# Gathered values, later weight loads and shared staging in a block-sparse attention and bilinear feed-forward kernel

## The chip, the cores and the metric

The kernel runs on one core of a Trainium2 chip. The metric is the device time of one execution in microseconds. A core has five engines that run beside each other, each through its own instructions in a fixed order: TensorE (PE, matrix products; its weight loads are shown as PEld), VectorE (DVE), ScalarE (ACT), GpSimd (POOL) and SyncE (SP, which here only issues DMAs). ScalarE and GpSimd issue DMAs too.

## The reference, cut to what matters

```
B, H, S, D = 4, 8, 768, 64                # blocks of 32 rows, 24 blocks
scores = q @ k.T / sqrt(D)
mask   = |bi - bj| <= 1, or bi or bj in (0, 23), or bj sampled for bi (3 of 24)
attn   = softmax(where(mask, scores, -1e9))
x      = (attn @ v) as [B*S, H*D]         # [3072, 512]
out    = ((x @ w_a) * (x @ w_b)) @ w_out  # weights are float64, d_ff = 1536
```

Keys and queries are some 4 times larger than values. A middle block attends to eight blocks: itself and its two neighbours, the first and the last, and three sampled ones. The first and the last block attend to all.

## The kernel before, in words

**Units of work.** A unit is one block of one batch, `attend(b, i)`, or `attend_all(b, i)` for blocks 0 and 23. Eight blocks are a chunk of 256 rows (3 chunks a batch, 12 in all). When a chunk's attention is done, its feed-forward products run: `first_products` (line 1429, 12 groups f of columns a chunk, 24 products each) and `second_products` (lines 1512 to 1514). Chunk 1 comes first, so the first eight units are blocks 8 to 15 of batch 0.

**Batch 0 in f32.** Its keys are loaded whole (`keys`, line 540, four DMAs on ScalarE's queue). Per unit GpSimd copies the eight key blocks into one of two tiles KG (lines 701 to 710; VectorE copies the near ones for the first two units). TensorE makes scores (975, with a mask product at 1120), VectorE the negated maxima (1135) and their product with 1/8 (1139), ScalarE the exponentials (1147), TensorE the transpose (1091), ScalarE its copy (1096), TensorE the sums with values (1043), VectorE the factor (1348 to 1356, tile xs), TensorE another transpose (1380), and ScalarE and VectorE write the chunk's rows xT (1391, 1392).

**Values of batch 0.** `gather_values` and `gather_after` fill one of two tiles VG by DMAs on SP's queue: three neighbour blocks (778), the first and last block when the tile changes batch (780, 781), three sampled ones (783). For the first eight units (`NEAR = 8`) the neighbours come instead by copies (745, `near_values`) from the resident values vp, which `plain_values_in` loads on ScalarE's queue (590) and of which it takes the maximum (600).

**Batches 1 to 3 in two f16 parts.** `keys` and `values` load a pair of heads into one of four places of the tile `stage` (546, 612), take its largest magnitude on ScalarE (558, 618), and scale it by a power of two: `set_scale` is a reduction over partitions on GpSimd (440) and three small VectorE operations (443 to 449). The scaled part and its remainder are made by ScalarE and VectorE (563, 564; 629, 630). Keys are transposed into keysT (573). Values are stored to DRAM (vd, 635) and gathered from there. For values the scale is one for all four pairs of a batch, so each pair keeps its place until all four maxima are known (`values_scale`, 645). Probabilities are split in two parts (1003 to 1010), transposed by DMA into one of three places pt (1187, 1291), and the result is factored (1348 on) and transposed by DMA into xT (1368).

**Weights.** `weights` loads 36 tiles of 512 KB with GpSimd's DMAs (898), at first into places of `stage` and of keysT[1]. `convert` makes f32 of the 64-bit words on VectorE (919, 922, 925), takes the maximum (939), and splits in two parts (946, 947). `weight_scale` sets the factor f1 (958, 961).

**Order.** All of it is written as generators that a planner (`Plan`) runs: each step has an engine, a cost in ns and a rank, and the planner emits the step that it reckons can begin first, weighed by rank. What it emits is each engine's fixed order. So any edit of a step, a cost or a number of places moves instructions on all engines.

```
W_BUFS = 6        RAW_BUFS = 4      VG_BUFS = 2
PT_BUFS = 3       NEAR = 8          KG_BUFS = 2
```

Of the kernel before, what the change touches and what calls it, by code (L numbers as in the profile page):

```python
# [48 lines left out]
LATE = 16  # L49
AT_ONCE = 4  # L50
NEAR = 8
# [243 lines left out]
def kernel(  # L295
# [43 lines left out]
    def take(tag, bufs):  # L339
        return rings.setdefault(tag, Ring(bufs)).take()  # L340
# [11 lines left out]
    stage = kvp.tile([P, RAW_BUFS, 2 * NT * D], F32, name="stage")  # L352
    keysT = [kvp.tile([P, H, S], F16, name=f"keysT{i}") for i in range(2)]
# [16 lines left out]
    n_at = at_g + NC  # L370
    bound = const.tile([P, n_at], F32, name="bound")
    bound_v = const.tile([P, B * NG], F32, name="bound_v")
# [16 lines left out]
    mark = const.tile([1, 1], F32, name="mark")  # L389
    offs = const.tile([1, NB, NR], I32, name="offs")  # L390
# [136 lines left out]
    def raw_tile(b, g, n):  # L527

        yield stage_freed
        t = stage[:, raw_taken[0] % RAW_BUFS]  # L530
        raw_taken[0] += 1
        freed = yield from take("raw", RAW_BUFS)
        return t, freed

    raw_taken = [0]

    def keys(b, g):
# [70 lines left out]
    def values(b, g):  # L608
# [18 lines left out]
        vs = work.tile([P, NT, 2, 2 * D], F16, tag="ks", name=f"vs{b}_{g}", bufs=KS_BUFS)  # L627
        s = scale[:, at_v + b : at_v + b + 1]
# [12 lines left out]

    def values_scale(b):
# [3 lines left out]
            bound[:, at : at + 1], bound_v[:, b * NG : b * NG + (NG if b else NT // 2)],  # L646
# [76 lines left out]

    def plain_vg(n):
# [29 lines left out]
    def gather_after(n):  # L754
        b, i, x = vg_units[n]
        vg_free[n] = yield from take("vg", VG_BUFS)
        if n + 1 < len(vg_units):
            plan.start(gather_values(n + 1), order[vg_units[n + 1][:2]] - LEAD_G)
        to, of, row = VG[n % VG_BUFS], vd[b], ROW
        if b == 0:  # L760
            to, of, row = plain_vg(n), plain_values, H * D
        dense = i in (0, NB - 1)
        first = vg_holds.get(n % VG_BUFS) != b
        vg_holds[n % VG_BUFS] = None if dense else b
# [119 lines left out]
    def weights(n):  # L884

        f, i = divmod(n, 3)
        if n == 0:
            yield from gate(W_GATE)
# [64 lines left out]
    def weight_scale(f):  # L953
# [670 lines left out]
```

## Time and profile before

| | |
|---|---|
| median of three executions | 807.28 us (803.25, 807.28, 808.39) |
| the profiled execution's own time | 803.08 us |
| its span, first to last instruction | 801.3 us |
| mean granted TensorE clock | 0.983 of 2.4 GHz |
| moved by DMA | 131.8 MB, mean 164 GB/s |

The profile shows one execution. Busy times of an engine leave out register, branch, semaphore and DMA-issuing instructions. An operation may begin before the one ahead of it on the same engine has ended, so the distance from one begin to the next is what it takes of the engine. "A <- B" is a wait of A that B ended. Lines are those of the kernel before.

### The profile page before, as it was taken

What the parts mean: (1) busy time and instruction counts of PE and PEld (TensorE: products, weight loads), DVE (VectorE), ACT (ScalarE), POOL (GpSimd) and SP (SyncE); (2) the same over time, 40 slices, a digit from 0 to 9 for tenths busy, and PEclk for the clock granted to TensorE, in tenths of its full rate; (3) what the DMA queues carried; (4) which work ended last, traced back from release to release, by engine and by line L of the source; (5) the groups of instructions that cost most, each with busy time, mean ns of one, the idle gap of its engine ahead of it and who ended that gap; (6) DMA issues with size and microseconds to landing.
All of it is one profiled execution on the core that took longest, in us unless ns stands there. A gap on an engine that the chain in (4) does not pass through costs nothing.

```text
span 801.3 us, 25888 instructions
## 1 busy us (share of the span) xinstructions
PE 742.4 (93%) x10056; PEld 522.5 (65%) x10056; DVE 533.6 (67%) x1504; ACT 490.9 (61%) x1202; POOL 227.6 (28%) x532
## 2 busy tenths in 40 slices
PE   2759789899998989999999999999989999999997
PEld 0426568674567748757758758658658757768853
DVE  5899999975666677676577686667667775322132
ACT  2666888786656677776466686565566664333333
POOL 5535833212233432202233432302234320000001
PEclk9879999999999999999999999999999999999999
DMA  8776786865577899897579998968687788310001
GB/s 270 234 215 196 228 249 189 266 131 135 126 186 163 182 197 226 179 231 155 144 180 170 214 239 170 210 172 171 155 179 164 147 158 167 91 34 1 2 1 53
DMA packets 184135, 131.80 MB, mean 164 GB/s; under 512 B 135627, under 2 KB 155724, under 8 KB 184012
## 3 DMA queue, kind: packets, MB, share of 16 engines
q1 hardware_dynamic: 170860, 82.89, 50.3%
q0 software_dynamic: 11616, 44.05, 17.5%
q10 hardware_dynamic: 1536, 3.21, 1.3%
q8 instruction: 79, 1.29, 0.7%
q14 instruction: 44, 0.36, 0.2%
HBM read 87.63 MB, written 11.01 MB: 123 GB/s over the span
## 4 chain that ended last, share of the span: by engine, by line
PE 65%; DVE 13%; DMA 9%; issue 5%; ACT 4%; SPq 3%; POOL 0%; POOLq 0%; ACTq 0%; DVEq 0%
PE ab L1429 37%; PE o L1512 6%; PE o L1514 5%; PE o L1513 5%; PE av L1043 5%; PE s L984 4%; DMA VG<-vd 4%; DMA vd<-vs 2%; DMA vp<-in_v_dram 2%; DVE low L1135 1%; SPq L666 1%; DVE wab L947 1%; SPq L783 1%; PE s L1120 1%; PE s L975 1%
## 5 line engine op out<-in xcount | busy, mean ns | idle before, releaser
L1429 PE MATMUL ab<-xT,wab 128*128 128x256 f16 x3456 | 393.2, 273 | 2.8 <-DVE g L1448 2.1
L1429 PEld LDWEIGHTS <-wab 128*128 128x128 f16 x3456 | 332.8, 98 | 58.1 <-issue 16.9
L1448 DVE TENSOR_TENSOR g<-g,ab 128x256 f32<-128x256 f32 x144 | 60.4, 419 | 112.9 <-ACT g L1445 109.3
L1445 ACT ACTIVATE g<-ab,f 128x256 f32<-128x256 f32 x144 | 67.7, 470 | 104.2 <-PE ab L1429 103.2
L1483 DVE SCALAR_TENSOR_TENSOR gh<-g,scale,gh 128x256 f16<-128x256 f32 x144 | 69.5, 494 | 72.0 <-ACT gh L1482 70.9
L1482 ACT ACTIVATE gh<-g,scale 128x256 f16<-128x256 f32 x144 | 70.7, 504 | 74.5 <-PE o L1514 70.6
L1512 PE MATMUL o<-wo,gh 128*128 128x512 f16 x288 | 110.1, 382 | 0.0
L1513 PE MATMUL o<-wo,gh 128*128 128x512 f16 x288 | 109.5, 380 | 0.0
L1514 PE MATMUL o<-wo,gh 128*128 128x512 f16 x288 | 109.5, 380 | 0.0
L710 POOL COPY KG<-keysT 128x128 int32 (+1 forms) x264 | 89.0, 375 | 44.6 <-POOL KG L701 22.5
L701 POOL COPY KG<-keysT 128x384 int32<-128x384 int32 (+1 forms) x86 | 50.6, 589 | 164.6 <-PE s L984 146.0
L1147 ACT ACTIVATE sm<-s,low,cq 128x256 f32<-128x256 f32 x132 | 73.6, 559 | 31.7 <-DVE low L1141 15.6
L440 POOL PARTITION_ALL_REDUCE power<-bound x58 | 25.8, 447 | 180.1 <-DVE bound L1462 103.7
L1043 PE MATMUL av<-VG,pt 128*32 128x128 f16 (+2 forms) x3488 | 63.5, 212 | 13.0 <-DMA VG<-vd 9.4
L1010 DVE SCALAR_TENSOR_TENSOR hl<-sm,hl 128x256 f16<-128x256 f32 (+1 forms) x156 | 69.8, 453 | 1.8 <-ACT hl L1003 0.5
L1135 DVE TENSOR_REDUCE low<-s 128x2 f32<-128x512 f32 x88 | 60.1, 683 | 14.9 <-PE s L984 12.0
L1043 PEld LDWEIGHTS <-pt 128*32 128x32 f16 x2688 | 33.1, 97 | 35.4 <-issue 26.6
L1512 PEld LDWEIGHTS <-gh 128*128 128x128 f16 x288 | 28.2, 98 | 36.9 <-issue 6.0
L1514 PEld LDWEIGHTS <-gh 128*128 128x128 f16 x288 | 28.2, 98 | 34.3 <-issue 0.5
L1513 PEld LDWEIGHTS <-gh 128*128 128x128 f16 x288 | 28.3, 98 | 29.1 <-issue 0.3
L1452 ACT ACTIVATE junk<-g 128x1024 f16<-128x1024 f32 x36 | 38.0, 1055 | 10.4 <-DVE g L1448 10.2
L1006 DVE TENSOR_SCALAR hl<-sm 128x256 f16<-128x256 f32 (+1 forms) x113 | 36.3, 325 | 11.7 <-DMA pt<-hl 8.9
(136 smaller groups left out, 932.3 us busy)
## 6 DMA issues: line engine op xcount, KB each, us to landing
VG<-vd SPq DMA_DIRECT2D x210, 64.0 KB, 3.0
VG<-vd SPq DMA_DIRECT2D x66, 192.0 KB, 3.7
q<-in_q_dram POOLq DMA_DIRECT2D x18, 512.0 KB, 4.9
VG<-vd SPq DMA_DIRECT2D x24, 384.0 KB, 3.7
out_dram<-ou POOLq DMA_DIRECT2D x24, 256.0 KB, 3.6
stage<-in_v_dram POOLq DMA_DIRECT2D x12, 384.0 KB, 4.5
vd<-vs SPq DMA_DIRECT2D x12, 384.0 KB
stage<-in_k_dram POOLq DMA_DIRECT2D x12, 384.0 KB, 6.5
```

What stands on the lines that cost most here:

```text
L710: nc.gpsimd.tensor_copy(to[:, :, (5 + r) * w : (6 + r) * w], of[:, :, bass.ds(at, w)])
L1010: t = yield dve(221 + n * 1.03, lambda: nc.vector.scalar_tensor_tensor(lo, sm, over, hi, ALU.mult, ALU.subtract))
L1043: mm(both[hs, :, i % 2, hq] if two else av[hs, i % 2, hq], pt[:, y, hs], of if two or b == 0 else of[:, 0], start=(i % 2 == 0 and hq == 0 ...
L1135: yield dve(685, lambda: nc.vector.tensor_reduce(mx, ps, axis=mybir.AxisListType.X, op=ALU.max, negate=True))
L1147: t = yield act(750, lambda hq=hq: nc.scalar.activation(sm[:, hq], ps[:, hq], AF.Exp, bias=low[:, at, hq, 0:1], scale=factor_of(b, cc, hq) ...
L1429: mm(ab[:, i, :].rearrange("p (j x q) -> p j x q", j=PER // 2, x=2), wab[:, f, i, part, kt, :], xc[:, :, a, :, kt, :], start=(i == 0 and k ...
L1445: yield act(460, lambda: nc.scalar.activation(g, ab[:, 0, :], AF.Copy, scale=f1[:, f : f + 1]))
L1482: yield act(400, lambda: nc.scalar.activation(gh[:, 0], g, AF.Copy, scale=s))
L1483: t = yield dve(480, lambda: nc.vector.scalar_tensor_tensor(gh[:, 1], g, s, gh[:, 0], ALU.mult, ALU.subtract))
L1512: mm(po, gh[:, 0, js], wo[:, f, 0], start=(f == 0), stop=False)
L1513: mm(po, gh[:, 0, js], wo[:, f, 1], start=False, stop=False)
L1514: mm(po, gh[:, 1, js], wo[:, f, 0], start=False, stop=(f == NF - 1))
```

## The change

- `NEAR = 0`: the neighbour values of the first eight units come by DMA gathers (778) like all others; `near_values` is no longer called.
- The first weight load waits until the second key tile has landed: a one-element GpSimd copy (`mark_w`) stands ahead of it.
- For batch 0 the product of the maxima with 1/8 goes from VectorE to ScalarE. f1 is made by one VectorE operation in place of two.
- Each pair of value heads has a scale of its own, set as soon as its own maximum is known. `values_even` takes the largest of the four and makes factors, `evened`, that the attention result's divisor takes in.
- `stage` has two places for keys and values in place of four. The room behind them is a third place for gathered values of batches 1 to 3, and a fourth for transposed probabilities.

```diff
+RAW_PLACES = 2
-NEAR = 8
+NEAR = 0
...
+    spare = stage.rearrange("p g x -> p (g x)")[:, RAW_PLACES * 2 * NT * D :]
...
-        t = stage[:, raw_taken[0] % RAW_BUFS]
+        t = stage[:, raw_taken[0] % RAW_PLACES]
-        freed = yield from take("raw", RAW_BUFS)
+        freed = yield from take("raw", RAW_PLACES)
...
+            if g == 1:
+                k_early.fire(t)
...
+        at = at_p + (b - 1) * NG + g
-            t, AF.Abs, accum_out=bound_v[:, b * NG + g : b * NG + g + 1],
-        ))
+            t, AF.Abs, accum_out=bound[:, at : at + 1],
+        ))
+        end = yield from set_scale(slice(at, at + 1))
         v_bound[b].fire(end)
         if g == NG - 1:
-            plan.start(values_scale(b), order[b, 0] - LEAD_V)
-        yield v_scale[b]
+            plan.start(values_even(b), order[b, 0] - LEAD_V)
...
-        s = scale[:, at_v + b : at_v + b + 1]
+        s = scale[:, at : at + 1]
...
+    def values_even(b):
+
+        yield v_bound[b]
+        at, to = at_p + (b - 1) * NG, at_v + b
+        yield dve(150, lambda: nc.vector.reduce_max(
+            rscale[:, to : to + 1], rscale[:, at : at + NG], axis=mybir.AxisListType.X
+        ))
+
+        def factors():
+            for x in range(2):
+                ps = slice(x * D, (x + 1) * D)
+                nc.vector.tensor_scalar(
+                    evened[ps, b], scale[ps, at : at + NG].rearrange("p (a i) -> p a i", i=2)[:, :, x],
+                    rscale[ps, to : to + 1], float(2.0 ** 14), ALU.mult, ALU.mult,
+                )
+
+        end = yield dve(320, factors)
+        v_scale[b].fire(end)
...
+    def split_vg(m):
+        at = vg_at[m]
+        if at < VG_BUFS:
+            return VG[at]
+        return spare[:, :ROW].bitcast(F16).rearrange("p (a x) -> p a x", a=2)
+
+    n_plain = sum(u[0] == 0 for u in vg_units)
+    vg_at = [m % VG_BUFS if m < n_plain else (m - n_plain) % 3 for m in range(len(vg_units))]
...
         if n == 0:
-            yield from gate(W_GATE)
+            yield k_early
+            yield pool(120, lambda: nc.gpsimd.tensor_copy(mark_w, plain_keys[0:1, 1, 0:1]))
...
-        end = yield dve(160, lambda: nc.vector.tensor_mul(
-            f1[:, f : f + 1], rscale[:, at : at + 1], rscale[:, at + 2 : at + 3]
-        ))
-        end = yield dve(160, lambda: nc.vector.tensor_mul(
-            f1[:, f : f + 1], f1[:, f : f + 1], rscale[:, at + 1 : at + 2]
+        end = yield dve(165, lambda: nc.vector.scalar_tensor_tensor(
+            f1[:, f : f + 1], rscale[:, at : at + 1], rscale[:, at + 1 : at + 2],
+            rscale[:, at + 2 : at + 3], ALU.mult, ALU.mult,
         ))
...
-            yield dve(165, lambda: nc.vector.tensor_scalar(mx, mx, D ** -0.5, None, ALU.mult))
+            yield act(200, lambda: nc.scalar.mul(mx, mx, D ** -0.5))
...
+    def place_pt(name, cols):
+        freed = yield from take("pt_split", PT_BUFS + 1)
+        at = pt_taken[0] % (PT_BUFS + 1)
+        pt_taken[0] += 1
+        if at == PT_BUFS:
+            yield stage_freed
+            t = spare[:, ROW : ROW + 4 * P].bitcast(F16).rearrange("p (a x) -> p a x", x=P)
+            return t[:, :cols], freed
+        return work.tile([P, cols, P], F16, tag="pt", name=f"pt{name}", bufs=PT_BUFS), freed
...
-            yield dve(165, lambda: nc.vector.tensor_scalar(
-                dn, dn, EPS, float(2.0 ** 14), ALU.add, ALU.mult
+            yield v_scale[b]
+            yield dve(165, lambda: nc.vector.scalar_tensor_tensor(
+                dn, dn, EPS, evened[:, b].unsqueeze(1).to_broadcast([P, 2, HQ]),
+                ALU.add, ALU.mult,
             ))
```

Lines in the orders are each kernel's own.

VectorE in the first units, before: 922 and 925 convert weights, 1135 and 1139 make maxima, 745 are the near copies into VG.

```order
L922 SCALAR_TENSOR_TENSOR wab<-keysT_77,wab 128x512
L1135 TENSOR_REDUCE low<-s_288 128x2
L745 COPY VG_84<-vp_115 32x512
L745 COPY VG_84<-vp_150 32x512 x2
L745 COPY VG_85<-vp_150 32x512 x3
L1139 TENSOR_SCALAR low<-low 128x2
L645 TENSOR_REDUCE bound<-bound_v 128x1
L925 SCALAR_TENSOR_TENSOR wab<-keysT_77,wab 128x512
L1135 TENSOR_REDUCE low<-s_319 128x2
L745 COPY VG_85<-vp_150 32x512 x3
L1348 TENSOR_SCALAR den<-den 128x4
```

The same place after: 970, 973 and 976 convert weights, 1184 makes maxima, 1407 and 1414 are the divisor.

```order
L1184 TENSOR_REDUCE low<-s_289 128x2
L970 TENSOR_SCALAR wo<-stage 128x512
L973 SCALAR_TENSOR_TENSOR wo<-stage,wo 128x512
L1407 TENSOR_SCALAR den<-den 128x4
L1184 TENSOR_REDUCE low<-s_317 128x2
L1414 RECIPROCAL den<-den 128x4
L976 SCALAR_TENSOR_TENSOR wo<-stage,wo 128x512
L1417 TENSOR_TENSOR xs_8_397<-av_8_323,den 128x256
L1184 TENSOR_REDUCE low<-s_403 128x2
```

The copies and the scalings of the maxima are gone from between the maxima. At the third and fourth unit's maximum the weights stand at the third tile (wo, from stage) where they stood at the fourth (wab, from keysT).

GpSimd at the start, before: 871 clears the queries' tile, 898 loads weights, 710 gathers sampled key blocks.

```order
L871 MEMSET QZ_112 64x1024 x2
L898 DMA stage<-in_moe_w_a_dram 128x1024
L898 DMA stage<-in_moe_w_b_dram 128x1024
L656 TENSOR_LOAD offs
L710 ISA
L710 COPY KG_82<-keysT_76 128x4x32
```

GpSimd at the start, after: 939 is the one-element copy that waits for the second key tile, 949 loads weights, 738 gathers key blocks.

```order
L921 MEMSET QZ_114 64x1024 x2
L939 COPY mark_w<-keysT_76 1x1
L949 DMA stage<-in_moe_w_a_dram 128x1024
L684 TENSOR_LOAD offs
L738 ISA
L738 COPY KG_82<-keysT_76 128x4x32
```

The second weight load (w_b) has left this place. It stands behind the copies of the first two units.

SP in batch 1, before: 778 and 783 gather values of a unit into VG, 1187 transposes a unit's probabilities, 1368 its output.

```order
L1187 DMA_TRANSPOSE pt_3595<-hl_3515 128x8x128
L778 DMA VG_84<-vd_79 96x1024
L783 ISA
L783 DMA VG_84<-vd_79 32x1024
L783 ISA
L783 DMA VG_84<-vd_79 32x1024
L783 ISA
L783 DMA VG_84<-vd_79 32x1024
L1187 DMA_TRANSPOSE pt_3750<-hl_3657 128x8x128
L1368 DMA_TRANSPOSE xT_86<-xo_0_3752 128x4x128
L778 DMA VG_85<-vd_79 96x1024
```

SP in batch 1, after: 828 and 833 gather values, 1429 transposes an output, 1235 probabilities; the gather into stage uses the third place.

```order
L833 DMA VG_85<-vd_79 32x1024
L828 DMA stage<-vd_79 96x1024
L694 TENSOR_LOAD offs
L833 ISA
L833 DMA stage<-vd_79 32x1024
L833 ISA
L833 DMA stage<-vd_79 32x1024
L833 ISA
L833 DMA stage<-vd_79 32x1024
L1429 DMA_TRANSPOSE xT_86<-xo_0_3719 128x4x128
L1235 DMA_TRANSPOSE stage<-hl_3721 128x8x128
L828 DMA VG_84<-vd_79 96x1024
```

Two gathers follow each other, the second ahead of the transposes, where a gather stood between transposes before.

## Rows read from the trace of the kernel before

**Rows 1.** The page, part 1: busy us, share of the span, instructions.

```profile
PE 742.4 (93%) x10056; PEld 522.5 (65%) x10056; DVE 533.6 (67%) x1504; ACT 490.9 (61%) x1202; POOL 227.6 (28%) x532
```

**Rows 2.** Table by stretch; the first row names the columns, after the stretch's length.

```profile
core 0: us, PE busy (x) PEld busy (x) DVE busy (x) ACT busy (x) POOL busy (x), PEclk, DMA share, GB/s
0.00:12.00 12.00, 0.35 (x4) 0.21 (x4) 3.51 (x22) 1.49 (x2) 3.27 (x8) 1.00 0.85 236
12.00:40.00 28.00, 20.38 (x286) 10.14 (x286) 24.18 (x57) 16.33 (x45) 18.30 (x42) 0.88 0.82 258
40.00:65.00 25.00, 14.85 (x230) 7.76 (x227) 24.46 (x69) 16.25 (x42) 8.28 (x17) 0.73 0.74 221
65.00:120.00 55.00, 46.83 (x780) 33.55 (x781) 54.76 (x134) 44.20 (x120) 34.93 (x68) 0.97 0.74 223
120.00:169.00 49.00, 46.80 (x611) 38.07 (x610) 44.94 (x119) 40.49 (x95) 13.78 (x27) 1.00 0.73 208
169.00:300.00 131.00, 122.20 (x1713) 79.21 (x1711) 87.84 (x262) 85.28 (x213) 42.91 (x109) 1.00 0.72 162
300.00:700.00 400.00, 394.79 (x5752) 285.78 (x5750) 268.50 (x781) 251.68 (x619) 102.19 (x256) 1.00 0.83 177
```

**Rows 3.** Waits of TensorE, 12 to 65 us: total us, times, longest.

```profile
PE av L1380 <- DVE xs L1356: 8.5, 3, 5.2
...
PE s L975 <- POOL KG L710: 4.9, 1, 4.9
```

**Rows 4.** The chain of waits, 12 to 66 us: start, us, what.

```profile
5.58 10.22 DMA vp<-in_v_dram
...
18.91 7.83 DMA vp<-in_v_dram
...
49.87 0.34 DVE wab L919
...
50.63 0.58 DVE wab L922
```

**Rows 5.** Groups of VectorE, 0 to 130 us: count, busy us, mean ns, idle before.

```profile
L745 DVE COPY VG<-vp 32x512 f32<-32x512 f32 x21 | 9.3, 443 | 0.5
```

**Rows 6.** Timeline of VectorE, 44 to 45 us: start, us, what.

```profile
44.24 0.15 DVE L1139 TENSOR_SCALAR low<-low 128x2 f32<-128x2 f32 x1
44.30 0.15 DVE L961 TENSOR_TENSOR f<-f,rscale 128x1 f32<-128x1 f32 x1
```

**Rows 7.** Timeline of GpSimd, 0 to 16 us.

```profile
2.64 0.68 POOL L898 DMA_DIRECT2D stage<-in_moe_w_a_dram  x1
3.32 0.55 POOL L898 DMA_DIRECT2D stage<-in_moe_w_b_dram  x1
12.63 0.88 POOL L710 COPY KG<-keysT 128x128 f32 x3 [8.76 <-DMA keysT<-in_k_dram]
...
15.25 0.53 POOL L898 DMA_DIRECT2D stage<-in_moe_w_out_dram  x1
```

**Rows 8.** The DMA view: 0 to 13 us in 40 slices, its queue q0; whole run's landing.

```profile
GB/s 0 0 0 0 0 2 180 95 255 340 370 360 355 380 321 380 429 385 293 243 230 221 277 233 233 202 271 214 325 217 236 310 241 271 276 331 266 364 389 399
...
q0 software_dynamic: 256, 0.97, 25.6%
...
stage<-in_moe_w_a_dram POOLq DMA_DIRECT2D x4, 512.0 KB, 4.7
```

**Rows 9.** Waits of TensorE, 169 to 700 us.

```profile
PE av L1043 <- DMA VG<-vd: 9.4, 8, 2.4
```

**Rows 10.** Timeline of ScalarE, 0 to 3 us.

```profile
2.04 0.20 ACT L1537 ACTIVATE warm<-warm 128x1 f32<-128x1 f32 x1
```

**Rows 11.** Staging: GpSimd's key loads and SP's value stores (timelines); landing of line 612.

```profile
275.93 1.10 POOL L546 DMA_DIRECT2D stage<-in_k_dram  x2
...
351.91 1.80 SPq L635 DMA_DIRECT2D vd<-vs  x2
...
DMA to landing us min/median/max: 3.7/4.5/5.9
```

More of the change, by code (lines that the diff above doesn't have):

```diff
@@ L369 @@
     at_g = at_w + 3 * NF
-    n_at = at_g + NC
+    at_p = at_g + NC
+    n_at = at_p + (B - 1) * NG
     bound = const.tile([P, n_at], F32, name="bound")
-    bound_v = const.tile([P, B * NG], F32, name="bound_v")
+    bound_v = const.tile([P, NT // 2], F32, name="bound_v")
+    evened = const.tile([P, B, HQ], F32, name="evened")
     power = const.tile([P, n_at], F32, name="power")
@@ L389 @@
     mark = const.tile([1, 1], F32, name="mark")
+    mark_w = const.tile([1, 1], F32, name="mark_w")
     offs = const.tile([1, NB, NR], I32, name="offs")
@@ L529, in raw_tile @@
         yield stage_freed
-        t = stage[:, raw_taken[0] % RAW_BUFS]
+        t = stage[:, raw_taken[0] % RAW_PLACES]
         raw_taken[0] += 1
-        freed = yield from take("raw", RAW_BUFS)
+        freed = yield from take("raw", RAW_PLACES)
         return t, freed
     raw_taken = [0]
+    k_early = Event()
     def keys(b, g):
@@ L645, in values_scale @@
         yield dve(150, lambda: nc.vector.reduce_max(
-            bound[:, at : at + 1], bound_v[:, b * NG : b * NG + (NG if b else NT // 2)],
+            bound[:, at : at + 1], bound_v,
             axis=mybir.AxisListType.X,
@@ L722, in gather_keys, with take_vg @@
         k_free[b].fire(t)
+    def split_vg(m):
[5 more added lines that the diff above has]
+    vg_at = [m % VG_BUFS if m < n_plain else (m - n_plain) % 3 for m in range(len(vg_units))]
+    vg_user = {}
+    def take_vg(m):
+        at = vg_at[m]
+        if at >= VG_BUFS:
+            yield stage_freed
+        ev = Event()
+        last = vg_user.get(at)
+        vg_user[at] = ev
+        if last is not None:
+            yield last
+        return ev
     def plain_vg(n):
@@ L755, in gather_after @@
         b, i, x = vg_units[n]
-        vg_free[n] = yield from take("vg", VG_BUFS)
+        vg_free[n] = yield from take_vg(n)
         if n + 1 < len(vg_units):
             plan.start(gather_values(n + 1), order[vg_units[n + 1][:2]] - LEAD_G)
-        to, of, row = VG[n % VG_BUFS], vd[b], ROW
         if b == 0:
             to, of, row = plain_vg(n), plain_values, H * D
+        else:
+            to, of, row = split_vg(n), vd[b], ROW
         dense = i in (0, NB - 1)
-        first = vg_holds.get(n % VG_BUFS) != b
-        vg_holds[n % VG_BUFS] = None if dense else b
+        first = vg_holds.get(vg_at[n]) != b
+        vg_holds[vg_at[n]] = None if dense else b
         def copies():
@@ L1183, in attend @@
         mine = yield from turn("pt", b, i)
-        kept = yield from take("pt", PT_BUFS)
+        pt, kept = yield from place_pt(f"{n}", 8)
         mine.fire(0)
-        pt = work.tile([P, 8, P], F16, tag="pt", name=f"pt{n}", bufs=PT_BUFS)
         t = yield sp(1300, 1500, lambda: nc.sync.dma_start_transpose(
@@ L1193, in attend @@
         yield from before(b, i)
-        vg = VG[m % VG_BUFS]
+        vg = split_vg(m)
         quads = [
@@ L1286, in attend_quad @@
             freed[x].fire(t)
-            kept = yield from take("pt", PT_BUFS)
+            pt, kept = yield from place_pt(f"{n}_{hq}{x}", 6)
             if x == 1:
                 mine_pt.fire(0)
-            pt = work.tile([P, 6, P], F16, tag="pt", name=f"pt{n}_{hq}{x}", bufs=PT_BUFS)
             t = yield sp(1100, 1130, lambda hl=hl, pt=pt: nc.sync.dma_start_transpose(
@@ L1315, in all_values @@
         else:
-            vg = VG[m % VG_BUFS].rearrange("p a x -> p (a x)")
+            vg = split_vg(m).rearrange("p a x -> p (a x)")
             terms = [
@@ L1329 @@
     ride = [Event() for _ in units]
+    pt_taken = [0]
+    def place_pt(name, cols):
[3 more added lines that the diff above has]
+        if at == PT_BUFS:
+            yield stage_freed
+            t = spare[:, ROW : ROW + 4 * P].bitcast(F16).rearrange("p (a x) -> p a x", x=P)
+            return t[:, :cols], freed
+        return work.tile([P, cols, P], F16, tag="pt", name=f"pt{name}", bufs=PT_BUFS), freed
     quad_sent = {(b, i): Event() for b in range(B) for i in (0, NB - 1)}
```

## The prediction

> **What bounds the kernel now.** I read the page first: TensorE is busy 93% of the span, VectorE 67%, ScalarE 61%, GpSimd 28% [rows 1]. The reader is to see there a kernel that is bound by its matrix products, in which only idle time of TensorE can be won. Both kernels issue the same products (10056 before; the order of after has as many of each kind), so the question is where the 59 us of idle stand (801.3 - 742.4) and who ends them.
>
> The table by stretch says where [rows 2]. TensorE stands idle 11.7 us in 0:12, 7.6 in 12:40, 10.2 in 40:65, 8.2 in 65:120, 2.2 in 120:169, 8.8 in 169:300, 5.2 in 300:700 and 5.8 at the end. So 40 us of 59 lie before 169 us, and in the same rows VectorE is busy 24.5 of 25, 54.8 of 55 and 44.9 of 49 us: from 40 to 169 us VectorE is the bound. It turns the int64 weights into two f16 parts there (36 tiles); the products of the first two chunks wait for the weights and for the attention output, which VectorE makes too.
>
> The waits of TensorE in 12:65 confirm it: 8.5 us for the output factor xs of VectorE, 4.9 us for the first gathered keys, which GpSimd could not copy before 12.6 us [rows 3]. The granted clock is 0.88 and 0.73 of 2.4 GHz in 12:40 and 40:65 [rows 2], so part of the time at 1.2 GHz, after stretches in which TensorE was idle; a higher clock alone would save nothing there, since VectorE sets the end, and I count nothing for it.
>
> Last I read the chain of waits. From 5.6 to 26.7 us it is two loads of the plain values vp [rows 4], and after them mostly VectorE. The near copies of the first eight blocks needed vp.
>
> **The change part by part.** Most of it takes work off VectorE ahead of 169 us.
>
> Near values: 24 copies of 32x512 go, 21 of which VectorE ran in 9.3 us with 0.5 us idle before them [rows 5]: -9.3 us of VectorE. In their place SP issues 8 DMAs of 192 KB (1.57 MB more to move), counted below.
>
> Scaled maxima: 22 small VectorE operations move to ScalarE. Each lasts 0.15 us, but the next begins 0.06 us after it began [rows 6], so one takes some 0.07 us of the engine: -22 x 0.07 = -1.5. The factor f1: one operation in place of two for 12 groups, -12 x 0.07 = -0.8. Scaling the values per head pair: four factors a batch in place of one, three VectorE operations each; up to the last weight the order of after has 10 more of these and the few that even them out: +0.9. The sum on VectorE up to the last weight is -9.3 - 1.5 - 0.8 + 0.9 = -10.7 us.
>
> On ScalarE the 22 operations cost 22 x 0.20 = 4.4 us, by the one row of so small an operation [rows 10]; three near copies go from it. ScalarE is busy 16.3 of 28 and 16.3 of 25 us in the stretches where most stand [rows 2], and the operation stands right ahead of the exponentials on the same engine, so a hop between engines goes as it comes. I take 0; without the cover it costs the 4.4. The Trainium skill (ScalarE: Activation LUTs, Rules for kernel authors) says the contrary: multiplications belong on VectorE, and a short ACTIVATE is budgeted at about 0.3 us; an estimate by that page is 22 x 0.3 = 6.6 us on ScalarE for 1.5 us saved. The trace agrees only in that ScalarE's is the longer operation (0.20 against 0.15).
>
> Weights behind keys: GpSimd now waits for the second key tile before its first weight load. Before, it issued w_a at 2.64 and w_b at 3.32 us, then stood until 12.63 and sent w_out at 15.25 [rows 7]; 0.97 MB of weights moved by 13 us, while the keys were landing [rows 8]. Behind the waiting instruction stand, in GpSimd's order, the load of w_a, the gathers of the first two key blocks, and only then w_b. At the some 300 GB/s of these slices 0.97 MB is 3.2 us: the keys land some 2.5 us earlier (not all of 3.2, since w_a follows the second key tile), at about 10 us, and with them the first scores. w_b then goes out 2.6 us later (12.63 to 15.25 for the same copies), at about 12.5 in place of 3.3 us, and lands after 4.7 us [rows 8] at 17; w_out follows at 21. So VectorE has less to do between 10 and 28 us: three tiles, of one operation of 0.34 and two of 0.58 us each [rows 4], are 4.5 us, and attention's own operations I estimate at as much again; that is 9 of 18 us, and 9 idle. Before, it was busy 24.2 of 28 us in 12:40, which is 2.5 idle in 18. The difference of 6.5, less 2.5 for the earlier keys, is +4. The bounds are 0 (the early tiles were not missed) and +9 (the whole delay of w_b). The 1.57 MB of gathers are 5 us at the same rate, in stretches where the DMA engines are 82% and 74% busy [rows 2]; that they hide is part of the 4, and that they don't is in the 9.
>
> The start therefore gains 10.7 - 4 = 6.7 us. What is late next there is VectorE still: it works 124 of the 129 us from 40 to 169 [rows 2].
>
> Values scaled per pair, GpSimd: 9 more small reductions over 500 us, on an engine busy 28%: 0. With them a pair is written out as soon as its own maximum is known, which lets a staging place go sooner; that pays for taking two of the four places away. I take 0 for both together; the price if it doesn't is below.
>
> Two more places: the room becomes a third place for gathered values and a fourth for transposed weights of attention. Between 169 and 700 us TensorE waits 9.4 us in 8 waits for gathered values [rows 9]; with a third place the gather of a block goes out a block earlier. The third pair of orders above shows a gather that no longer stands behind a transpose. The bounds are -9.4 and 0; some of these waits are SP's own queue, which is no shorter, so I take -4, a little under the middle. For the fourth place I take 0: among TensorE's waits I found none that it would end.
>
> **The sum.** -6.7 - 4.0 = -10.7 us. Against the profiled execution's own 803.08 us (span 801.3 and 1.8 around it) that is 792.4. The median of the three runs shown, 807.28, is 4.2 us above the profiled one; against it the sum gives 796.6. I forecast **796.5 us**. A measurement of this kernel tells about 1% (8 us) from no change.
>
> **The rivals.**
>
> *The gain at the start is given back.* The late weights and the 1.57 MB of gathers starve VectorE for the full 9 us, so 1.7 of its 10.7 remain; and the waits for gathered values were SP's queue, so a third place gives 2. Time: 807.3 - 3.7 = 803.6. For it: w_b goes out 9 us later, and the DMA engines are 82% busy in 12:40 [rows 2]. Against it: GpSimd's loads were held back by VectorE later on anyway, so a tile missed early is made up only if VectorE has idle time, which it hadn't after 40 us; and the chain up to 27 us [rows 4], the loads of vp, is gone.
>
> *Slower: two staging places hold up the next batch.* From the first key load of a batch to its last stored values it took 76 us, 275.9 to 351.9, for eight tiles through four places [rows 11]. Through two places each tile must turn within 76 / 4 = 19 us. A tile lands after 4.5 us [rows 11], and its five steps on three engines wait behind other work, since each engine keeps a fixed order. From 19 us a tile on, the next batch is late: at 22 us by 4 x 3 = 12 us, at two changes of batch 24 us, and 807.3 - 10.7 + 24 = 820.6. For it: the order of after loads the last two value tiles of a batch behind the first key gathers of that batch. Against it: the 76 us held the wait for all four maxima, which goes, and no wait of TensorE for keys or values at a change stands out now.
>
> *ScalarE's extra operations are on the path.* Each unit's chain then grows by 0.20 us at a place that nothing covers: 22 x 0.20 = 4.4 us, and 796.6 + 4.4 = 801.0. This is the rule of the Trainium skill above, at the trace's price. Against it: ScalarE is over a third idle there [rows 2].
>
> **How the numbers follow.** The forecast case gets 0.64, the gain given back 0.20, the two staging places 0.11, ScalarE 0.05. The forecast's own range is 791 to 803: VectorE's idle between +1 and +7, and the third place between -7 and -1, about its 796.6. Of its 0.64, 0.08 lies within 1% (above 799.2); the gain given back and ScalarE lie within 1% altogether; the two staging places are slower. So faster 0.56, same 0.33, slower 0.11. The range 786 to 809 leaves out the slower case and little else, under 0.2: its low end has both open terms at their best (10.7 + 9.4 = 20.1 off 807.3, and 1 more), its high end the gain given back with 5 us of gathers that don't hide.
>
> **What would show it.** Right: GpSimd's first key gather at about 10 us in place of 12.63; no near copy on VectorE; the last weight part on VectorE at about 162 us (before, the stretch that ends at 169 us ends with it); TensorE idle before that point down by 5 to 8 us; its waits for gathered values under 6 us. The late weights would show as VectorE idle of over 17 us in 0:40 (12.3 before). Wrong: VectorE full as before and the last weight where it was; new waits of TensorE for keys or gathered values at 330 to 360 and 500 to 530 us, when batches change; GpSimd standing before a load of keys or values.

## The result, and the profile after

The changed kernel takes 817.82 us (median of six, 811.49 to 826.18) against 807.32 us (median of six, 803.00 to 808.39): 1.0104 of the time before, 95% interval 1.006 to 1.0149; the ratio leaves out the execution of 826.18, which was in a slow state. The forecast was 796.5, its range 786 to 809. The profiled execution took 812.58 us, its span 810.8 (803.08 and 801.3 before).

Page, part 1, of the kernel after:

```profile
PE 742.2 (92%) x10056; PEld 525.0 (65%) x10056; DVE 516.3 (64%) x1469; ACT 496.3 (61%) x1234; POOL 228.4 (28%) x542
```

TensorE's work is that of [rows 1]; VectorE has 17.3 us less. The 9.5 us of span are idle time of TensorE, and the mean granted clock is 0.983 in both. The table by stretch of the kernel after says where it stands:

```profile
0.00:12.00 12.00, 0.35 (x4) 0.21 (x4) 4.28 (x25) 1.49 (x2) 3.51 (x11) 1.00 0.84 250
12.00:40.00 28.00, 19.84 (x310) 11.13 (x310) 16.87 (x37) 17.11 (x55) 17.68 (x43) 0.92 0.96 261
40.00:65.00 25.00, 16.62 (x275) 9.62 (x271) 23.72 (x61) 18.14 (x48) 10.63 (x20) 0.75 0.92 279
65.00:120.00 55.00, 48.10 (x759) 35.84 (x748) 52.99 (x122) 44.56 (x127) 32.87 (x67) 0.97 0.74 213
120.00:169.00 49.00, 46.33 (x603) 35.81 (x602) 43.56 (x117) 41.35 (x99) 14.72 (x27) 1.00 0.83 240
169.00:300.00 131.00, 119.73 (x1751) 79.20 (x1754) 89.74 (x265) 85.12 (x210) 45.27 (x113) 0.99 0.74 163
300.00:700.00 400.00, 385.50 (x5637) 279.40 (x5625) 256.41 (x776) 249.42 (x619) 99.74 (x256) 1.00 0.84 175
```

Against [rows 2]: up to 169 us TensorE's idle time went from 39.8 to 37.8 us, 2 us won where 6.7 were forecast. From 169 to 700 us it went from 14.0 to 25.8, 11.8 lost. VectorE's work up to 169 us fell by 10.4 us (151.85 to 141.43; forecast 10.7), but in 12:40 it is busy 16.9 of 28 us (24.2 before), and the DMA engines 96% and 92% in 12:40 and 40:65 (82% and 74%).

The DMA view of the kernel after (line's tiles, count, KB each, median us to landing), then its timelines of GpSimd and VectorE:

```profile
stage<-in_moe_w_a_dram POOLq DMA_DIRECT2D x4, 512.0 KB, 9.1
```

```profile
11.38 0.88 POOL L738 COPY KG<-keysT 128x128 f32 x3 [5.25 <-DMA keysT<-in_k_dram]
...
170.09 0.74 DVE L998 SCALAR_TENSOR_TENSOR wo<-w,scale,wo 128x512 f16<-128x512 f32 x1
```

The four loads of w_a into stage that landed in 4.7 us [rows 8] now need 9.1, and the last weight part ends at 170.8 us (168.8 before, forecast about 162). The first gather of keys moved only from 12.63 [rows 7] to 11.38. VectorE is idle 18.8 us in 0:40, over the 17 that were to show the late weights.

The last weight part before (VectorE's timeline of the kernel before), then a load of vp that is still in the chain of waits of after:

```profile
168.06 0.75 DVE L947 SCALAR_TENSOR_TENSOR wo<-w,scale,wo 128x512 f16<-128x512 f32 x1
```

```profile
8.92 9.62 DMA vp<-in_v_dram
```

Waits of TensorE after, 12:65 (first fence) and 169:700 (second):

```profile
PE av L1092 <- DMA VG<-in_v_dram: 7.0, 3, 3.7
...
PE s L1024 <- POOL KG L738: 4.1, 1, 4.1
PE av L1441 <- DVE xs L1417: 2.6, 2, 1.9
```

```profile
PE av L1092 <- DMA pt<-hl: 6.3, 8, 1.2
PE av L1092 <- DMA stage<-hl: 6.0, 3, 2.7
PE ab L1490 <- DVE g L1509: 5.2, 5, 1.7
```

At the start the waits for xs [rows 3] fell by 6 us and waits for gathered neighbours took their place. Later the 9.4 us for gathered values [rows 9] are gone, and 12.3 us of waits for transposed probabilities stand there. Before, the same view has:

```profile
PE av L1043 <- DMA pt<-hl: 0.5, 1, 0.5
PE ab L1429 <- DVE g L1448: 0.2, 1, 0.2
```

So SP's transfers together cost TensorE 12.3 us in place of 9.9. All waits of the view sum to 26.0 us in place of 13.6; the other 10 us of the difference are waits for VectorE (the feed-forward tile g above all, 5.2 against 0.2) and for ScalarE (6.5 against 2.0).

### The profile page after: what moved, and what is told of

It reads as the page before. It is cut to its first block, busy times and chain, and to the rows that moved or that the text cites. A ratio compares the mean times of both kernels' runs of the same rounds, so it can differ in the third digit from the quotient of the medians.

```text
span 810.8 us, 25904 instructions
## 1 busy us (share of the span) xinstructions
PE 742.2 (92%) x10056; PEld 525.0 (65%) x10056; DVE 516.3 (64%) x1469; ACT 496.3 (61%) x1234; POOL 228.4 (28%) x542
## 4 chain that ended last, share of the span: by engine, by line
PE 57%; DMA 15%; DVE 12%; ACT 6%; issue 6%; POOL 1%; SPq 1%; POOLq 0%; ACTq 0%
PE ab L1490 33%; PE o L1573 5%; PE o L1575 5%; PE o L1574 5%; PE av L1092 4%; PE s L1033 3%; DMA stage<-in_v_dram 3%; DMA pt<-hl 3%; DMA stage<-hl 2%; DMA keysT<-ks 2%; DMA vp<-in_v_dram 1%; DVE low L1184 1%; PE s L1024 1%; ACT sm L1196 1%; DVE g L1509 1%
## 5 line engine op out<-in xcount | busy, mean ns | idle before, releaser
L729 POOL COPY KG<-keysT 128x384 int32<-128x384 int32 (+1 forms) x86 | 48.4, 563 | 173.5 <-PE s L1033 149.3
L445 POOL PARTITION_ALL_REDUCE power<-bound x67 | 29.9, 448 | 211.5 <-DVE bound L1523 102.6
L1092 PE MATMUL av<-VG,pt 128*32 128x64 f32 (+2 forms) x2160 | 42.3, 220 | 11.5 <-DMA VG<-in_v_dram 7.0
L1513 ACT ACTIVATE junk<-g 128x1024 f16<-128x1024 f32 x36 | 38.0, 1057 | 12.2 <-DVE g L1509 11.9
L1055 DVE TENSOR_SCALAR hl<-sm 128x256 f16<-128x256 f32 (+1 forms) x100 | 30.8, 313 | 15.8 <-DMA stage<-hl 10.2
L1092 PEld LDWEIGHTS <-pt 128*32 128x32 f16 x2032 | 24.9, 97 | 24.7 <-issue 14.6
```

What stands on the lines that cost most here:

```text
L1092: mm(both[hs, :, i % 2, hq] if two else av[hs, i % 2, hq], pt[:, y, hs], of if two or b == 0 else of[:, 0], start=(i % 2 == 0 and hq == 0 ...
```

## The experiments

All ratios are to the kernel before, with a 95% interval. The theories, by the letters that the expectations use: **T**, the third place lets the planner put gathers ahead of transposes in SP's queue, and TensorE waits for these. **S**, the gathers fill the DMA engines at the start, and VectorE waits for loads instead of working less. **G**, the wait ahead of the first weight starves VectorE. **P**, any edit makes the planner write a new order, and a new order alone gives or costs about a per cent.

| run | ratio | interval | TensorE idle 0:169 | 169:700 |
|---|---|---|---|---|
| before | 1 | | 39.8 | 14.0 |
| after | 1.0104 | 1.0060 to 1.0149 | 37.8 | 25.8 |
| e1 | 1.0073 | 1.0038 to 1.0108 | 38.2 | 26.7 |
| e2 | 1.0015 | 0.9978 to 1.0053 | 40.5 | 18.7 |
| e3 | 1.0115 | 1.0076 to 1.0153 | 39.0 | 22.6 |
| e4 | 0.9971 | 0.9936 to 1.0007 | 37.7 | 19.8 |
| e5 | 0.9958 | 0.9926 to 0.9991 | 43.0 | 15.6 |
| e6 | 1.0102 | 1.0042 to 1.0161 | 36.4 | 25.9 |
| e7 | 0.9944 | 0.9890 to 0.9998 | 38.1 | 19.1 |
| e8 | 1.0038 | 1.0002 to 1.0074 | 38.6 | 25.4 |
| e9 | 1.0179 | 1.0130 to 1.0228 | 37.3 | 32.4 |
| e10 | 1.0072 | 1.0033 to 1.0111 | 34.4 | 25.4 |
| e11 | 1.0117 | 1.0082 to 1.0152 | 38.7 | 30.3 |
| e12 | 1.0189 | 1.0134 to 1.0244 | 39.3 | 29.6 |
| e13 | 0.9962 | 0.9932 to 0.9991 | 38.3 | 20.3 |
| e14 | 1.0030 | 0.9997 to 1.0063 | 40.0 | 22.9 |
| e15 | 1.0039 | 1.0008 to 1.0069 | 39.7 | 19.3 |
| e16 | 0.9974 | 0.9941 to 1.0007 | 38.7 | 16.2 |
| e17 | 1.0365 | 1.0312 to 1.0418 | 45.3 | 41.2 |
| e18 | 0.9972 | 0.9936 to 1.0008 | 37.9 | 16.0 |

Idle is 169 or 531 us less TensorE's busy time in the table by stretch. How far to trust it: e5 turned out to have the order of before on every engine, so it is a repeat of before, and came out at 0.9958, its idle time up to 169 us 3.2 us off. Differences under 0.5%, and of some 3 us in one profile's start, are not read below.

### The parts of the start (e1, e2, e3)

```diff
-NEAR = 0
+NEAR = 8                        # e1, e3
-            yield k_early
-            yield pool(120, lambda: nc.gpsimd.tensor_copy(mark_w, ...
+            yield from gate(W_GATE)     # e2, e3
```

> The changed kernel with NEAR = 8 again: near values by copies, all else changed. Theory S (the start is bound by DMA, which the gathers fill): DMA share in 12 to 65 us falls from 0.94 to under 0.85, weight loads land in 5 to 6 us in place of 8 to 9, but VectorE has its 9.3 us of copies again; last weight part at 167 to 171 us (170.8 in the changed kernel), time 808 to 816. Theory G (the late first weight load alone starves VectorE): landings and DMA share stay, last weight at 178 or later, time 820 or more.

> The changed kernel without the wait of the first weight load for the second key tile. Theory G (the wait costs VectorE its early tiles): VectorE's idle in 0 to 40 us falls from 18.9 to 14 or less and the last weight part comes at 163 to 166 us in place of 170.8; time 6 to 8 us under the changed kernel's. Theory S (DMA is full in 12 to 65 us whatever goes first): the early tiles come sooner, later ones later; last weight within 2 us of 170.8, time within 3 us of the changed kernel's.

> The changed kernel with both edits of the start undone (near copies back, no wait for keys); per-pair scaling, maxima on ScalarE, two more places stay. The start should be that of the kernel before, less 2 us of small VectorE operations: last weight at 165 to 169 us. If the middle (169 to 700 us) costs what the trace shows (idle 20.6 us against 14.0 before), the time is 5 to 9 us over the kernel before all the same; if the start alone is to blame, it is within 3 us of it.

The two undone parts do not add up: alone they give -0.3% and -0.9% against after, together +0.1%. In e1 the share of DMA in 12:65 fell to 0.81 (0.94 in after), as S had it, but the last weight part ended at 174.9 us, which neither theory has. In e2 VectorE was idle 12.2 us in 0:40 and the time fell by as much as G had it, but the last weight part came only at 168.7 us. e3 stayed as slow as after with the start undone. Each also made a new order, so none of them separates the part from the order.

### The third place (e4, e7), in another variant of the plan (e6, e8, e5)

```diff
-... (m - n_plain) % 3 for m in range(len(vg_units))]
+... (m - n_plain) % 2 for m in range(len(vg_units))]   # e4, e8
```

e7 keeps the three places in memory and lets the planner reckon with two, so its order is that of e4. e8 is e4 with the weights first. e5 and e6 are before and after with `HOP = 161` in place of 160; in e6 this moves a few instructions.

> The changed kernel with two places for gathered values of batches 1 to 3 in place of three; the fourth place for transposes stays. Theory T (gathers that go out a unit earlier fill SP's queue ahead of the transposes): TensorE's waits for transposes in 169 to 700 us fall from 12.3 to under 3, waits for gathered values come back with 6 to 10, time 3 to 6 us under the changed kernel's. Theory P (only the planner's new order is worse): both kinds of wait change by less than 3 us, and the time by less than 3.

> The changed kernel with three places in the chip's memory, but with the planner told of two, so that every engine's order is that of the run without the third place. Theory T (the order of SP's queue costs, not the place): waits for gathered values under 3 us (5.8 with two places), waits for transposes as with two places (about 4), time at or up to 4 us under the run without the third place. If the place itself costs (its writes into the staging tile), time and waits for transposes are those of the changed kernel, 12 us and 816 or more.

> The kernel before with one of the planner's constants off by one (HOP 161 ns in place of 160): the same operations, another order. It measures what a new order alone does. Theory P (re-planning scatters by as much as the change): 4 us or more from the kernel before, in either direction. If the order is robust, within 3 us.

> The changed kernel with the same constant off by one. Theory P: 4 us or more from the changed kernel, in either direction. Theory T (three places put gathers ahead of transposes in any plan): TensorE's waits for transposes in 169 to 700 us stay above 7 us and the time stays over the kernel before.

> The changed kernel without the weights' wait for keys and without the third place for gathered values. If both effects seen one by one (-0.9% and -1.3% against the changed kernel) add up: 798 to 802 us, under the kernel before. Theory P (each was a lucky order): 804 to 815.

With the planner's two places the kernel is 1.3% faster than after (e4), with the place itself kept 1.6% (e7): the place does no harm, the order made with it does. In e4 the waits for transposes fell to 3.9 us and those for gathered values came back with 5.8. That spoke for T. But in e7, where T put the waits for gathered values under 3 us, the view of 169:700 has

```profile
PE av L1096 <- DMA VG<-vd: 8.3, 8, 3.2
```

At the order of two places the third place ends none of these waits. And with the weights first, two places are no better than three (e8 1.0038, e2 1.0015). e6 stayed slow with 14.4 us of waits for transposes, but its order is so near that of after that it tells little.

### Only SP's queue, and two tests of the start (e9, e10, e11)

e9 keeps the orders of TensorE and VectorE as in after and issues the gathers of batches 1 to 3 behind the next transpose of probabilities:

```diff
-                nc.sync.dma_start(to[0 : 3 * BLK, 0, :], ...
+            held_back.append((n, issue))
...
+            nc.sync.dma_start_transpose(pt, hl.rearrange("p a h k -> p (a h k)"))
+            send_held()
```

> The kernel after with three places, and with TensorE's, VectorE's and ScalarE's order as in it; only on SP the gathers of values of batches 1 to 3 are issued behind the next transpose of probabilities instead of ahead of it (and at the latest ahead of the sums that read them). Theory T (the third place lets the gathers stand ahead of the transposes in SP's queue, and TensorE waits for these): TensorE's waits for transposes from 169 us on fall from 12.3 us to under 5, waits for gathered values come back with at most 8, and the time comes near that of the run with three places in the old order: ratio 0.994 to 1.002. Rival (the place in SP's queue does not matter, the other order on TensorE and VectorE does): ratio 1.006 to 1.013, and what waited for transposes waits for something else.

Waits of TensorE in e9, 169:700:

```profile
PE av L1109 <- DMA stage<-vd: 9.1, 6, 4.5
PE av L1109 <- DMA VG<-vd: 8.4, 8, 3.0
...
PE av L1109 <- DMA pt<-hl: 2.9, 3, 1.3
```

The waits for transposes fell from 12.3 to 3.2 (2.9 and 0.3 for those in stage), as T had it; but 17.5 us of waits for gathered values came back, and the time rose to 1.0179. The two kinds of transfer share one queue: in these two orders, whichever stood second was late. e9 holds each gather until the next transpose has been sent, which can be later than need be, so a milder order is not excluded. T's claim that putting the gathers second wins the time back fails in this plan; e13 and e14 below add another.

```diff
-            if not near:
+            if not near and not (b == 0 and 2 <= i < 8):                  # e10
-  nc.gpsimd.tensor_copy(mark_w, plain_keys[0:1, 1, 0:1])
+  nc.gpsimd.memset(mark_w, 0.0)                                           # e11
```

> The kernel after, same order, without the gathers of neighbour values for units 2 to 7 of batch 0 (6 of 192 KB, 1.2 MB; those units use what the place held before: that part of the computation is left out). Theory S (the 16 DMA engines are full from 12 to 65 us, so that what the gathers add delays the weights): the share of DMA in 12 to 65 us falls by 0.05 or more, the weights land some 4 us sooner (1.2 MB at the 270 GB/s moved there), the last weight part ends at 165 to 168 us, and the ratio falls to 1.003 to 1.007. Rival (the gathers are hidden; VectorE is held up by the order of weights alone): last weight part at 170 to 171 us and ratio 1.008 to 1.013.

> The kernel after, same order, but the copy ahead of the first weight's load writes a zero and reads no keys, so that the load is issued at about 3 us instead of 5.5. Theory S (DMA engines full anyway, so a transfer that starts sooner only displaces others): the keys land 1 to 2 us later, the first gather of keys is at 12 to 13.5 us, the last weight part stays at 169 to 171.5 us, and the ratio stays within 0.4% of that of after (1.006 to 1.014). Rival (the wait for the keys is what starves VectorE in the first 40 us): VectorE is busy 3 us more before 40 us, the last weight part ends at 165 to 167.5, ratio 1.002 to 1.006.

e10 missed its mark: chunk 1 comes first, so the gathers of blocks 2 to 7 are issued between 59 and 99 us in after, mostly behind the stretch that S speaks of. The share of DMA in 12:65 did not fall (0.98, 0.94 in after), and what moved less was 65:120 (188 GB/s against 213). The last weight part ended at 168.5 us and TensorE's idle time up to 169 us was 3.4 us lower, but 2.6 of these stood already before 65 us, so nothing is read from it. e11: the load without its wait changes nothing (1.0117; last weight part at 171.1). G falls in this order. The second weight load, w_b, still stands behind the copies of the first two units there, so e11 does not test its late start.

### New orders of the same instructions (e12, e13, e14; e17, e18)

```diff
-HOPS = {"PE": 200, "DVE": 140, "ACT": 130, "POOL": 130}
+HOPS = {"PE": 210, "DVE": 140, "ACT": 130, "POOL": 130}     # 230 in e17, e18
```

A constant of the planner alone, in before (e12, e17), in after (e13, e18), and in after with two places (e14).

> The kernel before with the planner's TensorE hop at 210 ns in place of 200: no instruction is added or removed, the order on all engines changes. Theory P (any new plan costs or gives about a per cent, and the plan of before is a good one by chance): ratio 1.003 to 1.015, TensorE's waits after 169 us above 17 us (13.6 before). Theory T (the third place is the cause; re-planning alone does little): ratio 0.996 to 1.003, waits 12 to 16 us.

> The kernel after (three places) with the same constant at 210 ns. Theory T: it stays slow, ratio 1.006 to 1.014, and slower than the two-place kernel with this constant by 1.0 to 1.7%; waits after 169 us at 24 us or more. Theory P: its time is drawn anew, 0.994 to 1.012, and the difference to the two-place kernel may have either sign.

> The kernel after with two places of values, and the constant at 210 ns. Theory T: ratio 0.993 to 1.000, as both runs of the two-place order gave; waits after 169 us at 18 to 21 us. Theory P: 0.996 to 1.012.

> The kernel before with the planner's TensorE hop at 230 ns: a third plan of the same instructions. Theory P (plans scatter by a per cent or more, and that of before lies at the good end): ratio 1.004 to 1.020. Rival (the plan at 210 was the odd one out): 0.995 to 1.004.

> The kernel after with the same constant at 230 ns, a third plan of it. Theory P: ratio 0.994 to 1.012, and the mean of its three plans at or below the mean of the three plans of before (1.010, 0.996 and this one against 1.000, 1.019 and that of the run before this). Rival (the change costs something in every plan, and 210 was lucky): 1.008 or more.

Before becomes 1.9% and 3.7% slower with not one step added or removed. After becomes 1.4% and 1.3% faster than it was. In the new order three places are faster than two (0.9962 against 1.003): the sign of the third place turns with the plan. P holds, and e12 and e17 lie even above what it expected; only its "any edit" goes too far, since e5 kept the order. Table by stretch and waits 169:700 of e17, then the table of e18:

```profile
0.00:169.00 169.00, 123.73 (x1793) 84.22 (x1794) 145.45 (x384) 113.88 (x293) 80.87 (x160) 0.90 0.72 222
169.00:700.00 531.00, 489.81 (x6969) 343.48 (x6967) 339.78 (x992) 325.18 (x799) 142.69 (x364) 0.98 0.78 163
```

```profile
PE av L1043 <- DMA VG<-vd: 20.5, 13, 4.0
PE av L1043 <- ACT pt L1096: 5.4, 4, 2.2
PE av L1043 <- DMA pt<-hl: 5.3, 5, 1.8
PE o L1512 <- ACT gh L1482: 4.4, 2, 3.5
```

```profile
0.00:169.00 169.00, 131.06 (x1931) 92.20 (x1932) 144.74 (x366) 124.64 (x333) 83.06 (x167) 0.92 0.83 239
169.00:700.00 531.00, 514.97 (x7427) 363.91 (x7428) 350.24 (x1038) 335.75 (x831) 146.29 (x367) 0.99 0.81 172
```

The loss of e17 sits in waits for SP's transfers and for ScalarE, spread over many units; e18, with all parts of the change, has as little idle time after 169 us (16.0) as before had (14.0). The waits for SP's two kinds of transfer together, in the three plans, are 9.9, 24.4 and 25.8 us in before, and 12.3, 9.2 and 7.0 in after.

### The gathers alone (e15), and at a fixed order (e16)

e15 is before with `NEAR = 0`. e16 lets the planner place the copies as before and emits nothing there, so every other instruction keeps its place:

```diff
-                for x in range(3):
-                    eng(to[x * BLK : (x + 1) * BLK, 0, :], plain_block(i - 1 + x))
+                pass
...
-            if not near:
+            if True:
                 nc.sync.dma_start(to[0 : 3 * BLK, 0, :], ...
```

> The kernel before with one part of the change alone: gathers in place of the copies of neighbour values (weights first, four raw places, two places of values, as before). By the step of the prediction (9.3 us of VectorE's copies go, 1.6 MB of gathers are hidden): ratio 0.987 to 0.992, last weight part at 159 to 161 us. Theory S (the 16 DMA engines become full from 12 to 65 us and hold VectorE up instead): ratio 0.996 to 1.004, last weight part at 165 us or later, the share of DMA in 12 to 40 us at 0.92 or more (0.82 before), and VectorE idle 3 us or more longer up to 65 us.

> The kernel before with its order held: the planner still places the copies of neighbour values, but nothing is emitted there (24 copies gone, 21 of VectorE's and 3 of ScalarE's), and the 8 gathers of neighbours stand in SP's queue ahead of those of sampled blocks; every other instruction keeps its place. By the step of the prediction (9.3 us of VectorE's work go, the gathers are hidden): ratio 0.987 to 0.992, TensorE's idle time up to 169 us 31 to 34 us (39.8 before). Theory S (the gathers fill the DMA engines in 12 to 65 us and VectorE waits instead): ratio 0.996 to 1.003, idle up to 169 us at 37 us or more, last weight part at 165 us or later.

Table by stretch of e16, waits of TensorE 12:65, waits of VectorE 12:65, the same of before, and pieces of the chain of waits of e16:

```profile
12.00:40.00 28.00, 18.15 (x238) 9.45 (x238) 19.01 (x51) 13.97 (x41) 18.18 (x42) 0.85 0.96 280
40.00:65.00 25.00, 19.27 (x275) 10.41 (x276) 21.28 (x55) 16.75 (x43) 8.23 (x16) 0.70 0.82 238
...
0.00:169.00 169.00, 130.29 (x1889) 90.68 (x1890) 140.96 (x374) 115.44 (x298) 78.10 (x160) 0.92 0.80 232
169.00:700.00 531.00, 514.85 (x7433) 364.14 (x7431) 354.35 (x1041) 335.36 (x829) 143.31 (x364) 1.00 0.80 174
```

```profile
PE av L1042 <- DMA VG<-in_v_dram: 6.8, 5, 2.6
PE s L974 <- POOL KG L710: 5.3, 1, 5.3
...
PE av L1379 <- DVE xs L1355: 0.5, 1, 0.5
```

```profile
DVE low L1134 <- PE s L974: 4.9, 3, 2.6
DVE KG L701 <- DMA keysT<-in_k_dram: 4.7, 1, 4.7
DVE bound L645 <- ACT va L600: 3.5, 1, 3.5
DVE xs L1355 <- PE av L1042: 3.3, 2, 2.7
```

```profile
DVE KG L701 <- DMA keysT<-in_k_dram: 4.3, 1, 4.3
DVE low L1135 <- PE s L975: 2.5, 3, 1.3
DVE wo L919 <- DMA stage<-in_moe_w_out_dram: 0.4, 1, 0.4
```

```profile
29.65 0.90 PE av L1042 x24
30.55 0.13 SPq L777
...
31.93 8.05 DMA VG<-in_v_dram
...
51.36 7.07 DMA VG<-in_v_dram
```

e16 is the change's largest part by itself. VectorE's work up to 169 us falls by 10.9 us (151.85 to 140.96), TensorE's idle time by 1.1. TensorE waited 8.5 us for xs [rows 3]; now 0.5 for xs and 6.8 for gathered neighbours. VectorE's waits in 12:65 are 16.7 us, against 7.2 in before: new are those for sums that wait for the gathers (3.3) and for the maximum of the values (3.5), which still needs the loads of vp [rows 4], and those for scores grew by 2.4. The share of DMA in 12:40 is 0.96, and the last weight part ends at 169.9 us. All of S's numbers came true at a fixed order. The ratio, 0.9974, leaves out the forecast's 0.987 to 0.992, though by less than the 0.4% that e5 was off; the idle time, 38.7 us where the forecast's step has 31 to 34, says it more clearly.

Whether full engines are the reason is only in part shown. In the chain above a unit's gathers go out at 30.55, once the sums that begin at 29.65 have freed one of the two places VG, and the next sums wait 8.05 us for the last of these gathers to land; a second such landing, of 7.07 us, follows. SP's own waits in 12:65 of e16 hold

```profile
SPq L777 <- PE av L1042: 14.0, 5, 3.9
```

That a gather can only start late is thus a second reason beside its taking long, and no run separates the two (a third place for batch 0 was not tried).

e15, with a new order, came out at 1.0039, within S, at a share of DMA of 0.98 in 12:40. Its last weight part ended at 165.4 us, 3.4 before that of before, and TensorE's idle time up to 169 us was the same (39.7 against 39.8): in that order TensorE got nothing of what VectorE gained.

On the DMA engines the Trainium skill (DMA: Bandwidth & Descriptors, Issuing engines are not separate DMA queues) says that transfers issued by any engine end up on the same 16 and interleave. The traces agree: the neighbours go out on SP, the weights on GpSimd's queue, and in e16, at the order of before, the four loads of w_a into stage land in 7.6 us in place of 4.7.

## Why the prediction was wrong, step by step

**VectorE's work: right in size.** Forecast -10.7 us up to the last weight, measured -10.4 up to 169 us (-8.6 up to the last weight part itself, which lies 2 us later and has other work before it). The 22 operations on ScalarE took 0.20 us each as forecast, 4.4 in all, and TensorE's waits for exponentials up to 169 us were 7.4 before and 6.8 after, which speaks against ScalarE's rival. The estimate of 6.6 us was by a budget that the Trainium skill (ScalarE: Activation LUTs, Rules for kernel authors) gives for operations whose bias is a pointer operand; the trace has 4.4, and no run here tries the move alone.

**"The start therefore gains 10.7 - 4 = 6.7": wrong.** It gained 2.0 (1.7 to 3.4 in e4, e6, e7 and e9, which keep all parts of the start). The step that failed is the +4 with its upper bound of +9 for VectorE's added idle time: VectorE's idle time up to 169 us rose by 10.4 us (17.2 to 27.6), beyond the bound, and its last weight part ended 2 us later. I had put that idle time down mostly to w_b's late start. In e16, where w_b goes out as early as before (3.32 us), the gathers alone add 10.9 us, so they suffice; what w_b's late start costs at a held order was not tried. I let 5 us of gathers hide in DMA engines that were 82% and 74% busy, by an average over the stretch, and did not ask what the sums and the weights would wait for. The earlier keys, put at 2.5 us, were 1.25. And "the chain, the loads of vp, is gone" was wrong: after's chain still has one of 9.62 us, since ScalarE and VectorE, each in its fixed order, still come to vp's maximum before later attention work (VectorE waits 3.5 us for it in e16). The rival of the gain given back named the gathers, and its 1.7 of 10.7 is near the 2.0 measured; its time, 803.6, was missed all the same, by what happened after 169 us.

**"-4 for the third place": the waits went, the time did not.** The waits for gathered values fell by all of 9.4 us. I had shown in the orders that a gather now stood ahead of a transpose, and priced only what that gives the gather; the bounds, -9.4 and 0, had no side for what it takes from the transposes. Their waits grew by 12.3 - 0.5 = 11.8 us, so of SP's transfers alone the term was +2.4 in place of -4. e9 shows the trade in the other direction, with both ends of it on one queue, and e7 (8.3 us of waits for gathered values) that it was the order and not the place that ended the waits. That the 11.8 us equal the idle time lost after 169 us is chance: the loss is these 2.4 and some 10 us of waits for VectorE and ScalarE, which the sum had no term for.

**The step that was missing: the new order itself.** The sum took the order of after as before's with some pieces moved. The planner wrote a new order for 700 us, and that alone was worth -1.4, -1.3, +1.9 and +3.7% in the four re-plans measured (two of each kernel), as much as all terms of the sum together (10.7 us, 1.3%) or more. The order of before is the fastest of its three, by 1.9%; that of after is the slowest of its three, by 1.3%. The 1.04% measured is one draw against another. The rival that ended slower, two staging places holding up the next batch, was not what happened: in 310:375 and 480:545 TensorE has no wait for keys or gathered values, and no single wait above 1.7 us. One reading of the prediction was off without effect: TensorE is idle 5.1 us at the end, not 5.8.

**What stays open.** Whether the change helps at like orders. The mean of the three plans is 1.0013 for after and 1.0185 for before, and at 210 and 230 ns after is faster than before by 2.2% and 3.8%; three draws with such a spread don't settle it. Of its parts three were tried at a fixed order, none told from 0: the gathers (e16, -0.3%), the third place (e7 against e4, -0.3%) and the wait ahead of the first weight (e11, +0.1% without it). The fourth place, the two staging places and w_b's late start were not tried alone. Why one order is better than another stays open too: the waits show where the time goes, not which of the planner's choices sent it there. The lowest ratio was that of e7, with all of the change and the order of two places: 0.9944, at the edge of what can be told from before.

## What to carry to other kernels

Where a planner sets the order, measure an edit at a held order (place the old step and emit nothing, or let the planner reckon with the old number of places) and measure the unchanged kernel under two or three neighbouring values of a planner's constant: the spread that this gives is the least that an edit's result must exceed to be the edit's. Work taken off the engine that sets the pace is worth only what its next input allows, so list for each operation that moves up what it will wait for, and take the transfer that replaces it as a load on everything that uses the same DMA engines there. A transfer that goes first in a queue puts another one second: price both.

## What the runs showed of the hardware

At a held order, with the neighbours' gathers added and the DMA engines' share up from 0.82 to 0.96 in 12:40 and from 0.74 to 0.82 in 40:65, the four 512 KB loads of w_a into stage took 7.6 us to land in place of 4.7 (e16). The 9.1 us of after have another part besides. Line 949 of after issues five such loads within 2.5 us from 45.2 us on, and they land after 5.1 to 11.2 us:

```profile
DMA to landing us min/median/max: 5.1/8.7/11.2
```

So a median over few loads can depend on how closely they were issued as well as on how busy the engines are. And a kernel whose engines are 93, 67, 61 and 28% busy lost 3.7% by the order of its instructions alone (e17), with no wait of TensorE above 5.5 us after the first 12 us.
